# Second feed-forward layer from reduced-float32 parts to float16 parts, in a fused attention and rational feed-forward kernel

## The chip, the cores and the metric

The kernel runs on one core of one Trainium2 chip. The metric is the device time of one execution in microseconds (us); lower is better. The kernel before took 1280.21 us (median of three runs, 1277.5 to 1283.15).

## What is computed

The reference first computes an attention with a threshold over 8 batches x 8 heads x 576 tokens of 64 elements, then a feed-forward network whose activation is a ratio of two polynomials:

```python
scores = scale * np.matmul(q, k.transpose(0, 1, 3, 2))
thresh = np.max(scores, axis=-1, keepdims=True) - tau
scores = np.where(scores >= thresh, scores, -1000000000.0)
...
x = np.ascontiguousarray(attn_out.transpose(0, 2, 1, 3)).reshape(B * S, H * D)
...
h = x @ w_in
...
P = a[0] + a[1] * h + a[2] * h2 + a[3] * h3
Q = 1.0 + np.abs(b[0]) * np.abs(h) + np.abs(b[1]) * h2
g = P / (Q + 1e-06)
return (g @ w_out).astype(np.float32)
```

`x` has 4608 rows of 512, `w_in` is 512 x 2048, `w_out` 2048 x 512. Everything is float32 outside, so each float32 matrix product inside is either a whole float32 product or a sum of three cheaper products of high and low parts (high x high, low x high, high x low).

## The kernel before

**Attention.** Heads are taken in pairs; a *unit* is 128 query rows of a pair (or the last 64 rows, "short rows"). A unit multiplies queries with keys on TensorE (PE, L805 to L816), takes row maxima on VectorE (DVE, L822 or L824, one instruction a unit, 160 in all), applies threshold and exponential on ScalarE (ACT, L837 and L841), splits the probabilities into float16 high and low parts (`hi` on ACT or DVE through a helper, L326 or L328; `lo` on DVE, L863), transposes them by DMA and multiplies with V (L934). The result is `x`, again in high and low float16 parts (L944, L950). Units of batch 0 use plain float32 for this.

**Feed-forward.** Tokens are taken in chunks of 256 columns (two a batch, kind `m`; the 64 short rows of four batches together make a chunk of kind `r`): 18 chunks. A *step* takes one chunk and four blocks of 128 of the 2048 hidden units. Its first layer is 48 float16 products of 256 columns (`f_g1`, L1051). The activation works on tiles `t` of 128 x 1024: scaling out of PSUM (ACT, L1060), absolute value (L1065 or L1067), polynomials on DVE (L1071, L1074, L1084), logarithm (ACT, L1078) and exponential (ACT, L1081) for the reciprocal, a correction of the reciprocal on DVE (L1087, L1090) and the last product (L1093). The second layer (`f_g2`) adds into two PSUM banks of 128 x 512, one a half of the tokens: of four blocks, one is a whole float32 product a half (L1114) and three are products of three parts in the reduced float32 type `fp32r` (L1110). The parts of the activation are made block by block: a high part of 256 columns (`f_gh`, helper lines L318 on ACT, L320 on DVE) and a low part of 256 columns (`f_gl`, DVE, L1101), in tiles `g`. The program has 71 steps of four blocks and two of two blocks, 73 entries.

**Weights** come as 64-bit words and are decoded on the core during the first part of the program, in four groups of 512 hidden units. `w_in` is measured block by block (`junk`, L544 on ACT or L546 on DVE), a group's maximum goes through PE to all partitions (`scale_ops`, L422 to L440), and blocks are scaled and split into float16 halves (helpers L326 and L328, and L562). Of `w_out`, 4 of 16 blocks are decoded and kept; 12 are cast to `fp32r` (L318 or L320) and subtracted (L592).

**Order.** All operations are entered in a list with durations, due times and the buffers that they take; a planner (`Plan.order`) runs through them once at build time and writes each engine's instructions in the order in which they start in its plan. Where an operation may run on ACT or DVE (`FLEX`), the planner picks. Due times of steps come from `LEAD`, `SPACING` and their like; the list `LAST` names the chunks whose steps are due after all attention. Engines then run their own order and wait for one another by semaphores. Loads of q, k and v in later batches are issued from GpSimd's queue (POOL).

## Time and profile before

| what | value |
|---|---|
| median of the runs | 1280.21 us |
| the profiled execution itself | 1281.68 us |
| its span, first to last instruction | 1279.9 us |
| mean granted TensorE clock | 0.994 |
| time of the last max reduction's start (L822 or L824) | 1133 us |

The rows of the profile that the prediction rests on are shown there. A group's row gives line, engine, operation, tiles, shape and count, then its busy us and the mean ns of one, then the idle time before them and what ended it. Matmul records of whole float32 products come in twos. Rows of the table of stretches give a stretch, its length, and for each engine the busy us and the instructions in brackets, then the granted clock, the share of the DMA engines and GB/s.

### The profile page before, as it was taken

What the parts mean: (1) busy time and instruction counts of PE and PEld (TensorE: products, weight loads), DVE (VectorE), ACT (ScalarE), POOL (GpSimd) and SP (SyncE); (2) the same over time, 40 slices, a digit from 0 to 9 for tenths busy, and PEclk for the clock granted to TensorE, in tenths of its full rate; (3) what the DMA queues carried; (4) which work ended last, traced back from release to release, by engine and by line L of the source; (5) the groups of instructions that cost most, each with busy time, mean ns of one, the idle gap of its engine ahead of it and who ended that gap; (6) DMA issues with size and microseconds to landing.
All of it is one profiled execution on the core that took longest, in us unless ns stands there. A gap on an engine that the chain in (4) does not pass through costs nothing.

```text
span 1279.9 us, 25127 instructions
## 1 busy us (share of the span) xinstructions
PE 1246.4 (97%) x9252; PEld 889.8 (70%) x9252; DVE 1199.3 (94%) x1960; ACT 1074.5 (84%) x2180; POOL 231.3 (18%) x480
## 2 busy tenths in 40 slices
PE   8899999999999999999999999999999999999998
PEld 6576676676767667766667667677776667677775
DVE  5899999999999999999999899999999999997876
ACT  5999888989999888888897699999988998874454
POOL 2112000132132311332022140322121221100000
PEclk9999999999999999999999999999999999999999
DMA  7645246688667656776442765876566665530000
GB/s 216 174 143 163 78 105 112 134 144 154 105 133 132 146 107 119 142 137 126 91 105 56 131 141 111 142 135 136 104 120 125 130 123 112 111 71 17 18 17 17
DMA packets 338251, 146.64 MB, mean 115 GB/s; under 512 B 314416, under 2 KB 320720, under 8 KB 338128
## 3 DMA queue, kind: packets, MB, share of 16 engines
q1 hardware_dynamic: 316528, 87.67, 38.5%
q0 software_dynamic: 21280, 56.78, 16.4%
q8 instruction: 73, 1.20, 0.4%
q10 hardware_dynamic: 320, 0.59, 0.2%
q14 instruction: 50, 0.41, 0.1%
HBM read 60.30 MB, written 9.44 MB: 54 GB/s over the span
## 4 chain that ended last, share of the span: by engine, by line
PE 53%; DVE 27%; ACT 8%; issue 5%; DMA 3%; SPq 0%; DVEq 0%; ACTq 0%
PE banks L1051 16%; PE banks L1110 15%; PE banks L1114 6%; PE banks L934 6%; PE banks L816 5%; DVE e L863 4%; DVE st L822 3%; DMA pT<-e 2%; DVE t L1071 2%; DVE t L1087 2%; DVE t L1090 2%; PE banks L805 2%; DVE t L1084 2%; DVE t L1093 2%; DVE g L1101 2%
## 5 line engine op out<-in xcount | busy, mean ns | idle before, releaser
L1051 PEld LDWEIGHTS <-wi 128*128 128x128 f16 x3456 | 324.1, 98 | 144.1 <-issue 108.0
L1051 PE MATMUL banks<-x,wi 128*128 128x256 f16 x3072 | 374.7, 275 | 3.0 <-ACT t L1060 1.7
L1110 PE MATMUL banks<-wp,g 128*128 128x512 f32 x1296 | 355.2, 415 | 1.9 <-ACT g L318 1.2
L1110 PEld LDWEIGHTS banks<-wp,g 128*128 128x128 f32 x1296 | 234.0, 189 | 70.9 <-issue 15.5
L837 ACT ACTIVATE e<-banks,st 128x576 f32<-128x576 f32 x288 | 206.4, 735 | 18.5 <-DVE st L831 11.1
L841 ACT ACTIVATE e<-e,cf 128x576 f32<-128x576 f32 x288 | 221.0, 774 | 0.3
L863 DVE SCALAR_TENSOR_TENSOR e<-e,st,hi 128x576 f16<-128x576 f32 x252 | 203.5, 808 | 3.9 <-ACT hi L326 3.4
L822 DVE TENSOR_REDUCE st<-banks 128x2 f32<-128x1152 f32 x128 | 171.8, 1342 | 12.9 <-PE banks L816 10.8
L326 ACT ACTIVATE hi<-e,st 128x576 f16<-128x576 f32 x177 | 134.0, 769 | 51.9 <-DVE st L852 41.1
L816 PE MATMUL banks<-KK,QQ 64*128 64x512 f32 x512 | 144.5, 641 | 0.0
L1114 PE MATMUL banks<-wp,t 128*128 128x512 f32 x288 | 142.2, 608 | 1.7 <-DVE t L1093 1.6
L1060 ACT ACTIVATE t<-banks,hsc 128x512 f32<-128x512 f32 (+1 forms) x192 | 106.3, 575 | 25.9 <-PE banks L1051 24.7
L934 PEld LDWEIGHTS <-V 128*64 128x64 f16 x2520 | 104.1, 111 | 33.8 <-issue 32.6
L934 PE MATMUL banks<-pT,V 128*64 128x256 f16 (+1 forms) x2520 | 118.9, 249 | 3.0 <-DMA pT<-e 3.0
L1087 DVE SCALAR_TENSOR_TENSOR t<-t,co,t 128x1024 f32<-128x1024 f32 (+1 forms) x73 | 92.0, 1261 | 22.7 <-ACT t L1081 22.7
L1078 ACT ACTIVATE t<-t,co 128x1024 f32<-128x1024 f32 (+1 forms) x73 | 82.7, 1133 | 12.8 <-DVE t L1084 12.7
L1093 DVE SCALAR_TENSOR_TENSOR t<-t,co,t 128x1024 f32<-128x1024 f32 (+1 forms) x73 | 92.0, 1261 | 0.5
L1071 DVE SCALAR_TENSOR_TENSOR t<-t,co 128x1024 f32<-128x1024 f32 (+1 forms) x73 | 92.0, 1260 | 0.0
L1084 DVE SCALAR_TENSOR_TENSOR t<-t,co,t 128x1024 f32<-128x1024 f32 (+1 forms) x73 | 91.9, 1260 | 0.0
L1074 DVE SCALAR_TENSOR_TENSOR t<-t,co 128x1024 f32<-128x1024 f32 (+1 forms) x73 | 91.9, 1259 | 0.0
L1101 DVE TENSOR_TENSOR g<-t,g 128x256 fp32r<-128x256 f32 x216 | 86.6, 414 | 2.0 <-ACT g L318 1.6
L1090 DVE SCALAR_TENSOR_TENSOR t<-t,t 128x1024 f32<-128x1024 f32 (+1 forms) x73 | 87.7, 1201 | 0.4
(137 smaller groups left out, 1518.2 us busy)
## 6 DMA issues: line engine op xcount, KB each, us to landing
KK<-in_kT_dram POOLq DMA_DIRECT2D x84, 144.0 KB, 3.9
t<-in_w_in_dram POOLq DMA_DIRECT2D x16, 512.0 KB, 5.8
t<-in_w_out_dram POOLq DMA_DIRECT2D x16, 512.0 KB, 4.7
V<-in_v_dram POOLq DMA_DIRECT2D x24, 256.0 KB, 4.4
out_dram<-u POOLq DMA_DIRECT2D x24, 256.0 KB, 2.7
QQ<-in_qT_dram POOLq DMA_DIRECT2D x42, 144.0 KB, 3.1
QQ<-in_qT_dram POOLq DMA_DIRECT2D x42, 128.0 KB, 3.4
KK<-in_kT_dram SPq DMA_DIRECT2D x24, 144.0 KB, 3.5
```

Of the source, the lines that this page charges most:

```text
L326: nc.scalar.activation(dst, src, AF.Identity, scale=factor)
L816: nc.tensor.matmul(d, QQ[r, t * P:(t + 1) * P], KK[r, REM:S], **one)
L822: nc.vector.tensor_reduce(box["st"][:, 0:2], box["both"], AX.X, ALU.max, negate=True)
L837: nc.scalar.activation(ev(hh), box["s"][hh], AF.Prelu, scale=SCALE, bias=box["st"][:, 2 + hh:3 + hh], alpha=STEEP)
L841: nc.scalar.activation(e, e, AF.Exp, scale=passes, accum_out=box["st"][:, 4 + hh:5 + hh])
L863: nc.vector.scalar_tensor_tensor(box["lo"][:, c], ev(hh), box["st"][:, 6 + hh:7 + hh], box["hi"][:, c], ALU.mult, ALU.subtract)
L934: nc.tensor.matmul(dst, V[:, c * P + head * D:c * P + (head + 1) * D], rhs, start=c == 0 and n == 0, stop=c == NT and n == 2)
L1051: nc.tensor.matmul(d, wi_tile(c, f0 + j, hl), x[:, c, :], start=c == 0 and n == 0, stop=c == NC - 1 and n == 2)
L1071: nc.vector.scalar_tensor_tensor(box["r"], box["h"], a2, box["h"], ALU.add, ALU.mult)
L1087: nc.vector.scalar_tensor_tensor(box["q"], box["q"], qc, box["i"], ALU.add, ALU.mult)
L1110: nc.tensor.matmul(acc[tt], fr(g[:, x]), fr(wo[f][y]), start=begins and j == n == 0, stop=ends and j == nb - 1 and n == 2)
L1114: nc.tensor.matmul(acc[tt], box["r"][:, o:o + P], wo[f], start=begins and j == 0, stop=ends and j == nb - 1)
```

## The change

**Second layer.** `w_out` is now measured, scaled by group and split into float16 halves in the way of `w_in`; block 0 of each group is kept in scaled float32 as well (`wp`). In most steps block 0 stays a whole float32 product and the other three are three float16 products each; in the last 13 entries all four blocks are in float16 parts. The parts of the activation are made by one instruction for three blocks (768 columns) or for all four (1024).

**Scales.** For float16, the activation needs a scale that can't overflow. It is a bound: the greatest column norm of `w_in` (`f_columns`, four products of a row of ones with the squares, per group) times the scale of the chunk's rows goes through the polynomial's absolute coefficients (`f_bound` on POOL, `f_scales` on DVE), and its logarithm enters the exponential as a bias (`f_inv`). A run of steps of one kind and batch and group range has one such scale (12 runs). The correction (`f_n`) takes a tile's scalar where it had a constant, and the output's scale becomes `down`.

**Sizes.** Blocks of `w_in` and half of `w_out`'s groups are measured by a sum of squares on ACT, the rest by a maximum on DVE; V's batches 1 to 7 by squares on ACT.

**Order.** Only one chunk of the last batch is left in `LAST`, and short rows of batch 7 come with the first visit of its pairs. Eleven tiles `t` in place of eight; all times of the table and the planner's prices have other values.

```diff
+WHOLE, IN_PARTS = 1, 13
...
+STEPS = {'m': (4, 4, 4, 4), 'r': (4, 4, 4, 4), 'last': (4, 4, 4, 2, 2)}
+LAST = (1,)
+
+REST_FIRST = (7,)
...
-PARTS = 3
+SQUARES_W, SQUARES_V = (2, 3), (1, 2, 3, 4, 5, 6, 7)
...
-LEAD, SPACE0, SPACING = 4.776489494, 2.7365, 2.085146464
+LEAD, SPACE0, SPACING = 5.323779532, 2.637044739, 2.235134465
...
-    wo = [None] * NF
+    wo = wpool.tile([P, NW, NC, 2, WS], F16, name="wo")
+    wp = wpool.tile([P, NW, WHOLE, WS], F32, name="wp") if WHOLE else None
...
+            def size(n=n, box=box):
+                if plan.eng == "ACT":
+                    nc.scalar.activation(box["rw"][:, :, 0].bitcast(F32), box["w"], AF.Square, accum_out=wm[:, n:n + 1])
+                else:
+                    nc.vector.tensor_reduce(wm[:, n:n + 1], box["w"], AX.X, ALU.max, apply_absolute_value=True)
+            o7 = op({"ACT": 0.66} if squares else {"DVE": 0.62}, 0, key, size, [o6], (), [hold])
...
+        sd = scale_ops(key, lambda: wm[:, n:n + NC], 14 - o, inv, sc, [x[3] for x in pieces], AHEAD_RANK, squares, EVEN if o else MASK)
...
+            def f_columns():
+                for c, box, _, _ in pieces:
+                    nc.tensor.matmul(bank(hb), ones16, squared(box["rw"]), start=c == 0, stop=c == NC - 1)
...
+        for c, box, hold, _ in pieces:
+            def s1(c=c, box=box):
+                times(dst(c, 0), box["w"], sc)
+
+            def s2(c=c, box=box):
+                nc.vector.scalar_tensor_tensor(dst(c, 1), box["w"], sc, dst(c, 0), ALU.mult, ALU.subtract)
+            o1 = op(FLEX["s1"], 0, key, s1, [sd], (), [hold])
+            wd.append([op(FLEX["s2"], 0, key, s2, [o1], (), [hold])])
+            if o and c < WHOLE:
+                wd[-1].append(op(FLEX["s1"], 0, key, lambda c=c, box=box: times(wp[:, i, c], box["w"], sc), [sd], (), [hold]))
...
-        def f_wh(f=f, box=box):
-            copy(fr(wo[f][0]), box["w"])
-
-        def f_wl(f=f, box=box):
-            nc.vector.tensor_tensor(fr(wo[f][1]), box["w"], wo[f][0], ALU.subtract)
-        o = op(FLEX["wh"], 0, key, f_wh, [o], (), [hold])
-        wo_done.append(op("DVE", 0.66, key, f_wl, [o], (), [hold]))
...
+        if bb in REST_FIRST:
+            visits += [(v0 + i, half + rest) for i in range(NP - 1)] + [(v0 + NP - 1, half + rest + other)]
+            visits += [(v0 + i, other) for i in range(NP - 2, -1, -1)]
...
-        def f_inv():
-            nc.scalar.activation(box["i"], box["i"], AF.Exp, scale=-1.0)
+        def f_inv(x, j0, j1):
+            i = box["i"][:, j0 * CT:j1 * CT]
+            nc.scalar.activation(i, i, AF.Exp, scale=-1.0, bias=lnr(x))
...
-        def f_n():
-            nc.vector.scalar_tensor_tensor(box["q"], box["q"], -2.0, box["i"], ALU.add, ALU.mult)
+        def f_n(x, j0, j1):
+            q, i = (box[y][:, j0 * CT:j1 * CT] for y in "qi")
+            nc.vector.scalar_tensor_tensor(q, q, m2r(x), i, ALU.add, ALU.mult)
...
-        def f_gh(j):
-            box["g", j] = place(hg[j])
-            copy(fr(box["g", j][:, 0]), box["r"][:, j * CT:(j + 1) * CT])
-
-        def f_gl(j):
-            g = box["g", j]
-            nc.vector.tensor_tensor(fr(g[:, 1]), box["r"][:, j * CT:(j + 1) * CT], g[:, 0], ALU.subtract)
+        def f_gh(x, j0, j1):
+            box["g", x] = place(hg[x])
+            copy(box["g", x][:, 0, 0:(j1 - j0) * CT], box["r"][:, j0 * CT:j1 * CT])
+
+        def f_gl(x, j0, j1):
+            w = (j1 - j0) * CT
+            nc.vector.tensor_tensor(box["g", x][:, 1, 0:w], box["r"][:, j0 * CT:j1 * CT], box["g", x][:, 0, 0:w], ALU.subtract)
...
-            if in_parts(f):
-                g = box["g", j][:, :, tt * P:(tt + 1) * P]
-                for n, (x, y) in enumerate(((0, 0), (1, 0), (0, 1))):
-                    nc.tensor.matmul(acc[tt], fr(g[:, x]), fr(wo[f][y]), start=begins and j == n == 0,
-                                     stop=ends and j == nb - 1 and n == 2)
+            x = f // NC
+            if f % NC < whole:
+                o = j * CT + tt * P
+                nc.tensor.matmul(acc[tt], box["r"][:, o:o + P], wp[:, x, f % NC], start=begins and j == 0, stop=ends and j == nb - 1)
                 return
-            o = j * CT + tt * P
-            nc.tensor.matmul(acc[tt], box["r"][:, o:o + P], wo[f], start=begins and j == 0, stop=ends and j == nb - 1)
+            o = (f - max(x * NC, f0) - whole) * CT + tt * P
+            for n, (y, z) in enumerate(((0, 0), (1, 0), (0, 1))):
+                nc.tensor.matmul(acc[tt], box["g", x][:, y, o:o + P], wo[:, x, f % NC, z], start=begins and j == n == 0,
+                                 stop=ends and j == nb - 1 and n == 2)
...
+            def f_bound():
+                x = isx[:, b:b + 1] if kind == "m" else R
+                e = engines[plan.eng]
+                e.tensor_scalar(H, x, wmax, 1.0, ALU.mult, ALU.mult)
+                e.tensor_scalar(s, H, c2, H, ALU.add, ALU.mult)
+                e.tensor_scalar(s, s, c1, H, ALU.add, ALU.mult)
+                e.tensor_scalar(s, s, c0, ct, ALU.add, ALU.mult)
+
+            def f_scales():
+                nc.vector.scalar_tensor_tensor(s, H, c1s, s, ALU.add, ALU.min)
+                nc.vector.tensor_single_scalar(s.bitcast(I32), s.bitcast(I32), EVEN, ALU.bitwise_and)
+                nc.vector.tensor_scalar(s, s, SMALL, None, ALU.max)
+                nc.vector.tensor_scalar(R.bitcast(I32), s.bitcast(I32), -0.5, float(197 << 23), ALU.mult, ALU.add)
+                nc.vector.tensor_scalar(m2r, m2, R, None, ALU.mult)
+                nc.vector.tensor_scalar(down, s, dn, None, ALU.mult)
+
+            def f_ln_r():
+                nc.scalar.activation(lnr, m2r, AF.Ln, scale=-0.5)
...
+    order += [(x, 0, NF) for i, x in enumerate((("m", B - 1, 0), ("m", B - 1, 1), ("r", B // 4 - 1, 0))) if i not in LAST]
...
+    for i, (ck, f, nb, p, begins, ends, gs) in enumerate(todo):
+        moe_ops(ck, f, nb, p, begins, ends, i >= len(todo) - SOON, WHOLE if nb % NC == 0 and i < len(todo) - IN_PARTS else 0, gs)
```

How this moves instructions is seen at three places. First, ACT in the early part, while the weights of the second layer come in (`u`, `t`: decoding; `wp`, `wo`: weights; `e`, `pT`: attention). Before:

```order
L493 ACTIVATE u_78<-t_71 128x512
L499 ACTIVATE t_71<-t_71 128x512
L318 CAST wp_0_148<-t_73 128x512
L493 ACTIVATE u_76<-t_75 128x512
L318 CAST wp_0_150<-t_71 128x512
L499 ACTIVATE t_75<-t_75 128x512
```

The same stage of the changed kernel:

```order
L879 ACTIVATE e_73<-banks,st_81 128x576
L531 ACTIVATE u_70<-t_96 128x512
L339 ACTIVATE wo<-t_96,so 128x512
L331 COPY pT_76<-banks 128x4x128
L339 ACTIVATE wo<-t_99,so 128x512
L879 ACTIVATE e_73<-banks,st_81 128x576
L883 ACTIVATE e_73,st_81<-e_73,cf 128x576
```

A scaled half (`wo`), which waits for its group's scale (`so`), stands in the place of a cast, between the two exponential chains of a unit.

Second, DVE at the end of a group of the second layer's weights (`sc`: the group's maximum; `st`, `u<-ident`: attention). Before:

```order
L503 TENSOR_SCALAR u_76<-u_76 128x512
L333 ISA t_70<-t_70,u_78 128x512x2
L333 ISA t_74<-t_74,u_76 128x512x2
L320 CAST wp_0_155<-t_70 128x512
L427 TENSOR_SCALAR u_78<-ident,sc_95 128x128
L592 TENSOR_TENSOR wp_1_156<-t_70,wp_0_155 128x512
L592 TENSOR_TENSOR wp_1_158<-t_74,wp_0_157 128x512
```

In the changed kernel:

```order
L467 TENSOR_REDUCE sc_86<-banks 128x1
L469 TENSOR_SCALAR sc_86<-sc_86 128x1
L470 TENSOR_SCALAR sc_86<-sc_86 128x1
L474 TENSOR_SCALAR so<-sc_86 128x1
L476 RECIPROCAL so<-so 128x1
L1136 SCALAR_TENSOR_TENSOR t_94<-t_94,co 128x1024
L341 TENSOR_SCALAR wp<-t_96,so 128x512
L613 SCALAR_TENSOR_TENSOR wo<-t_96,so,wo 128x512
L613 SCALAR_TENSOR_TENSOR wo<-t_97,so,wo 128x512
L613 SCALAR_TENSOR_TENSOR wo<-t_99,so,wo 128x512
L613 SCALAR_TENSOR_TENSOR wo<-t_95,so,wo 128x512
```

The low parts of the four blocks now come together behind the chain that makes the group's scale.

Third, PE in the second layer of a step (`wp`, `wo`: weights; `g`: parts; `t`: whole activation). Before:

```order
L1110 MATMUL banks<-wp_0_145,g_97 128x512 x2
L1110 MATMUL banks<-wp_1_146,g_97 128x512
L1110 MATMUL banks<-wp_0_145,g_97 128x512 x2
L1110 MATMUL banks<-wp_1_146,g_97 128x512
L1114 MATMUL banks<-wp_147,t_74 128x512 x2
L812 MATMUL banks<-KK_115,QQ_113 128x2x64
```

In the changed kernel:

```order
L854 MATMUL banks<-KK_116,QQ_114 128x2x64
L858 MATMUL banks<-KK_116,QQ_114 128x512 x2
L1164 LDWEIGHTS g_89
L1164 MATMUL banks<-wo,g_89 128x512
L1164 LDWEIGHTS g_89
L1164 MATMUL banks<-wo,g_89 128x512
```

Each float16 product has a load of its own for its stationary part. Counted over the whole order, 1296 reduced-float32 products and 144 whole ones became 1368 float16 products and 120 whole ones. On DVE, 60 of the 73 entries begin ahead of the last max reduction before, and 61 in the changed kernel.

More of the change, by code (lines that the diff above doesn't have):

```diff
@@ L410, in masked_attention_rational_ffn, with bounds, scale_ops @@
     co = op("DVE", 2.1, 6.0, monic, [co])
-    def scale_ops(key, get, up, inv, s, after, ahead=0.0):
+    def bounds():
+        nc.vector.tensor_single_scalar(co_[:, 9:12].bitcast(I32), co_[:, 0:3].bitcast(I32), 0x7FFFFFFF, ALU.bitwise_and)
+        nc.vector.tensor_scalar(c1s, ct, 1.0, 0.25, ALU.add, ALU.mult)
+        nc.vector.scalar_tensor_tensor(c1s, c1s, c1, c2, ALU.mult, ALU.add)
+        nc.vector.scalar_tensor_tensor(c1s, c0, ct, c1s, ALU.mult, ALU.add)
+    co_b = op("DVE", 0.4, 6.0, bounds, [co])
+    def scale_ops(key, get, up, inv, s, after, ahead=0.0, squares=False, mask=MASK):
         box = {}
@@ L670, in is_plain @@
     def is_plain(bp, t):
-        return bp < NP and t in PLAIN
+        return t in PLAIN.get(bp, ())
     v_ops = {}
@@ L1028, in moe_ops, with can, slow, mid @@
         FW = nb * CT
+        parts = [(x, max(x * NC, f0) - f0, min(x * NC + NC, f0 + nb) - f0) for x in range(g, (f0 + nb - 1) // NC + 1)]
         box = {}
-        def can(kind):
-            return {e: size(e, d) for e, d in FLEX[kind].items() if e == "DVE" or not soon}
-        def size(e, d):
-            return d + (nb / 2 - 1) * (d - {"ACT": 0.18, "DVE": 0.08}[e])
-        def on(e, d, *rest):
-            return op(e, size(e, d), *rest)
+        def can(n, act, dve):
+            return {"DVE": dve(n)} if soon else {"ACT": act(n), "DVE": dve(n)}
+        def slow(n):
+            return 0.129 + n * 0.2667
+        def mid(n):
+            return 0.068 + n * 0.2667
+        def fast(n):
+            return 0.07 + n * 0.1333
+        def act(n):
+            return 0.098 + n * 0.2133
         bhs = [Hold("b", 1 if kind == "m" else 4, BH if p < end else BH + [(i,) for i in B3[0]]) for _ in range(nb // 2)]
@@ L1123, in f_o @@
                     o = o[:, tt * DM:(tt + 1) * DM]
-                nc.scalar.activation(o, acc[tt], AF.Identity, scale=osc)
+                nc.scalar.activation(o, acc[tt], AF.Identity, scale=down)
             obox[tt]["o"] = o
@@ new lines, in scale_of, with f_top @@
+    def scale_of(ck, gs):
+        kind, b, _ = ck
+        run = kind, b, gs
+        if run not in scales_of:
+            n = len(gs)
+            done, m2, wmax, dn = consts(gs)
+            tab = const.tile([P, 2 * n + 4], F32, name=f"gs_{kind}{b}_{gs[0]}_{n}")
+            m2r, lnr = tab[:, 0:n], tab[:, n:2 * n]
+            H, s, R, down = (tab[:, 2 * n + i:2 * n + i + 1] for i in range(4))
+            def f_top():
+                nc.vector.tensor_reduce(R, isx[:, 4 * b:4 * b + 4], AX.X, ALU.max)
+            def f_bound():
[14 more added lines that the diff above has]
+                nc.scalar.activation(lnr, m2r, AF.Ln, scale=-0.5)
+            bs = [b] if kind == "m" else range(4 * b, 4 * b + 4)
+            p = max(pos[(x * NP, 0)] for x in bs) + 1.5
+            rank, plan.rank = plan.rank, p
+            o = [done] + [isx_done[x] for x in bs]
+            if kind == "r":
+                o = [op("DVE", 0.08, p, f_top, o)]
+            o = op(BOUND, 0, p, f_bound, o)
+            o = op("DVE", 0.8, p, f_scales, [o])
+            o = op("ACT", 0.25, p, f_ln_r, [o])
+            plan.rank = rank
+            scales_of[run] = o, lnr, m2r, down
+        o, lnr, m2r, down = scales_of[run]
+        return o, lambda x: lnr[:, x - gs[0]:x - gs[0] + 1], lambda x: m2r[:, x - gs[0]:x - gs[0] + 1], down
```

318 lines of the change are left out of this document (178 added, 140 removed).

## The prediction

> **What bounds the kernel now.** I read the page first: the busy line, for which engines are near full.
>
> ```profile
> span 1279.9 us, 25127 instructions
> PE 1246.4 (97%) x9252; PEld 889.8 (70%) x9252; DVE 1199.3 (94%) x1960; ACT 1074.5 (84%) x2180; POOL 231.3 (18%) x480
> ```
>
> Two engines are nearly full and a third is not far off, so an average decides nothing. The second view is the table of stretches. I cut it where DVE starts its 8th, 16th, 24th and 32nd max reduction (62.6, 121.5, 184 and 241.2 us) and its last one, the 160th (1133 us), because the order of the changed kernel can be cut at the same places. Columns: length, then busy us (and instructions) of PE, weight loads, DVE, ACT, POOL.
>
> ```profile
> 0.00:62.60 62.60, 51.67 (x332) 38.57 (x334) 43.24 (x120) 47.47 (x105) 14.28 (x44) 0.97 0.69 198
> 62.60:121.50 58.90, 56.72 (x446) 41.46 (x443) 57.08 (x138) 57.81 (x125) 10.26 (x22) 1.00 0.48 142
> ...
> 241.20:1133.00 891.80, 880.74 (x6735) 620.32 (x6735) 865.15 (x1362) 789.76 (x1610) 201.24 (x403) 1.00 0.63 122
> 1133.00:1279.92 146.92, 140.86 (x898) 106.38 (x895) 117.11 (x146) 73.02 (x129) 0.00 (x0) 0.99 0.10 25
> ```
>
> Three stages with different limits. **Early**, with the weights decoded, ACT and DVE are both full (57.81 and 57.08 of 58.90). **Middle**: DVE 865.15 and PE 880.74 of 891.80; DVE has 26.7 us idle in all. **Tail** (the feed-forward steps left over when attention is done): PE has 6 us idle and DVE 29.8, so PE bounds it. The waits of DVE after 1133 us say the same: it stands waiting for the exponential, whose input comes from the product that PE has just made.
>
> ```profile
> DVE t L1087 <- ACT t L1081: 18.9, 10, 2.4
> ```
>
> Third, the chain that ended last gives the pace of each kind of product, where PE runs without a break (start, length, matmul records):
>
> ```profile
> 1132.92 9.17 PE banks L1051 x84
> 1142.09 1.72 PE banks L1114 x4
> 1145.12 2.80 PE banks L1110 x12
> ```
>
> First-layer float16 of 256 columns: 9.17/84 = 0.109 us. Whole float32: two records each, so 1.72/2 = 0.86 us a product. Reduced-float32 parts of 512 columns: 2.80/12 = 0.233 us.
>
> **The change, part by part.** Base: the profiled execution took 1281.7 us, span 1279.9; the median of the three runs is 1280.2, so I take 1.5 off at the end.
>
> *PE.* A full step (4 blocks, 2 token halves) costs 48 x 0.109 + 18 x 0.233 + 2 x 0.86 = 11.15 us now. No row has a float16 product of 512 columns. Its bounds: 0.109 (as for 256) and 0.233 (as the one it replaces); I take twice the 256-column row, 0.219, since both work row by row. Then a mixed step costs 5.23 + 18 x 0.219 + 1.72 = 10.9 (-0.25), and a step all in parts, which the last 13 entries are (12 full steps' worth), 5.23 + 24 x 0.219 = 10.5 (-0.65). The Trainium skill, "TensorE: Matmul & The Clock Gate", section "Back-to-back issue gap", gives 262 cycles for 256 columns and 518 for 512, about 216 ns, but also a sustained 131 ns for 512. Our row agrees with the first (0.109); by the second the step would cost 8.4 us.
>
> *Early: second-layer weights.* Counted in the order, over all weights: sizes of blocks on ACT 11 to 24, on DVE 5 to 8; scaled halves on ACT 6 to 22, on DVE 10 to 14; 16 new low halves on DVE for 12 subtractions; 12 casts (4 on ACT, 8 on DVE) go.
>
> ```profile
> L544 ACT ACTIVATE t<-t 128x512 f32<-128x512 f32 x11 | 7.6, 692 | 3.1 <-DVE t L333 3.1
> L544 ACT ACTIVATION_READ_ACCUMULATOR t<-t 128x1 f32 x11 | 2.3, 207 | 0.0
> L326 ACT ACTIVATE wi<-t,sw 128x512 f16<-128x512 f32 x6 | 4.6, 781 | 0.0
> L318 ACT CAST wp<-t 128x512 fp32r<-128x512 f32 x4 | 2.8, 688 | 0.3 <-DVE t L333 0.2
> L562 DVE SCALAR_TENSOR_TENSOR wi<-t,sw,wi 128x512 f16<-128x512 f32 x16 | 11.6, 745 | 0.0
> L592 DVE TENSOR_TENSOR wp<-t,wp 128x512 fp32r<-128x512 f32 x12 | 8.2, 683 | 0.1
> L320 DVE CAST wp<-t 128x512 fp32r<-128x512 f32 x8 | 3.5, 436 | 0.0
> L328 DVE TENSOR_SCALAR wi<-t,sw 128x512 f16<-128x512 f32 x10 | 4.5, 478 | 0.0
> L546 DVE TENSOR_REDUCE wm<-t 128x1 f32<-128x512 f32 x5 | 3.4, 680 | 0.0
> L427 DVE TENSOR_SCALAR u<-ident,sc 128x128 f32<-128x128 f32 x12 | 3.4, 281 | 0.0
> L437 DVE TENSOR_SCALAR sc<-sc 128x1 f32<-128x1 f32 x12 | 1.8, 153 | 0.4
> ```
>
> ACT: 13 x 0.90 + 16 x 0.78 - 2.8 = +21. DVE: 16 x 0.745 - 8.2 - 3.5 + 4 x 0.478 + 3 x 0.68 = +4.2; four more scale chains (two of 0.28 and five of 0.15 each), four column norms (0.68 and three of 0.15) and three tables of constants (seven of 0.15) are 5.3 + 4.6 + 3.2 = 13, in all +17. Together about +38, some 20 on each engine. Nothing hides it: both are full from 62.6 to 121.5. **+20 us**. Bounds: +10 if half of it finds the idle of the first 62.6 us (ACT 15, DVE 19), +40 if the two take turns. The added wait: no half of a group is written before all four blocks are sized and PE has broadcast their maximum; queued behind those halves on ACT are the exponentials of attention, and DVE waits for these. The bound of each run (four tiny operations on POOL) stands ahead of loads of q, k and v, in a queue that is 18% busy: nothing.
>
> *Middle, DVE.* How far instructions overlap is seen where three follow each other:
>
> ```profile
> 1184.70 1.28 DVE L1071 SCALAR_TENSOR_TENSOR t<-t,co 128x1024 f32<-128x1024 f32 x1
> ...
> 1185.90 1.28 DVE L1074 SCALAR_TENSOR_TENSOR t<-t,co 128x1024 f32<-128x1024 f32 x1
> ...
> 1187.09 1.28 DVE L1084 SCALAR_TENSOR_TENSOR t<-t,co,t 128x1024 f32<-128x1024 f32 x1
> ```
>
> They start 1.20 apart and last 1.28, so one costs its mean less 0.08. The rows touched:
>
> ```profile
> L1101 DVE TENSOR_TENSOR g<-t,g 128x256 fp32r<-128x256 f32 x216 | 86.6, 414 | 2.0 <-ACT g L318 1.6
> L320 DVE CAST g<-t 128x256 fp32r<-128x256 f32 x93 | 25.7, 285 | 2.2 <-PE banks L1110 1.5
> L318 ACT CAST g<-t 128x256 fp32r<-128x256 f32 x123 | 47.8, 401 | 41.9 <-PE banks L1110 35.7 <-DVE t L1093 5.3
> L1087 DVE SCALAR_TENSOR_TENSOR t<-t,co,t 128x1024 f32<-128x1024 f32 x71 | 90.5, 1276 | 22.7 <-ACT t L1081 22.7
> L1090 DVE SCALAR_TENSOR_TENSOR t<-t,t 128x1024 f32<-128x1024 f32 x71 | 86.3, 1215 | 0.4
> L328 DVE TENSOR_SCALAR hi<-e,st 128x576 f16<-128x576 f32 x75 | 38.0, 513 | 0.2
> L326 ACT ACTIVATE hi<-e,st 128x576 f16<-128x576 f32 x177 | 134.0, 769 | 51.9 <-DVE st L852 41.1
> ```
>
> Low parts: 216 of 256 columns become 60 of 768, 11 of 1024, 2 of 512. From 0.414 (256) and 0.683 (512, L592) the slope gives 0.95 and 1.22: 72.1 to 65.9, -6. High parts on DVE: 93 to 28 + 4 + 1, by 0.285 and 0.436, 19 to 17, -2 (ACT, by 0.401 and 0.688, -9). The step whose constant becomes a tile's scalar goes from L1090's price to L1087's: 73 x 0.06 = +4. High halves of attention, 18 fewer: -8 on DVE, +14 on ACT. Twelve runs' scales, six tiny operations each: +10. Copies and sizes of V that go to ACT: -3. Sum -5; the same addition over the order between max reductions 32 and 160 gives -13 for equal steps. I take -9. But one step more, 8.6 us (six at 1.2, low parts 0.87, part of the casts), stands ahead of the last max reduction (61 entries of 73, not 60): **0**.
>
> What PE's relief adds there is idle time that DVE loses: between 0 and 26.7. PE asks 52 x 0.25 = 13 less, and DVE waits where both queues interlock; I take **-10**.
>
> *Tail.* PE bounds it. 12 steps' worth stand behind the last max reduction now, 11 after: -11.15 - 11 x 0.65 = -18.3, and with PE's 6 idle kept, **-19**. DVE, 117.11 less a step, asks 108 and has some 20 left as cover. The new order of the last batch moves chunks, not work; that one step is all that it yields here, and the stores stay 30 on POOL's queue and 10 on SP's.
>
> Sum: 1281.7 + 20 + 0 - 10 - 19 = 1272.7, less 1.5: about **1272 us**.
>
> **The rivals.** *PE is the pace of the middle too, and the weights' work hides* (PE's 97% speaks for it, ACT's 57.81 of 58.90 against): all of PE's saving falls through, 1296 x 0.014 + (24 x 0.86 - 72 x 0.219) - 4 of added column sums = 19; 1261. *No gain in the middle*: DVE at 865 of 892 was the wall and keeps its idle: 1280.2 + 20 - 19 = 1281, no change. *Slower: the early stage takes turns.* Each group's maximum is one more round over DVE, PE and DVE, and while ACT scales halves, attention's exponentials stand still and DVE with them; the extra 40 us then add up in one line: 1280.2 + 40 - 19 - 10 = 1291, 1301 with no idle recovered. It decides from an early growth of 36 us (26 without recovery): the 32nd max reduction after 277 us instead of 241. *The product does not get cheaper*, 0.233 as before: the tail gives 15 instead of 19, 1276. *It gets far cheaper*, down to the 256-column row: the tail is left to DVE, 108 plus some 7 of waits in place of 127, 12 less: 1260. By the sustained 131 ns of the Trainium skill, "TensorE: Matmul & The Clock Gate", "Back-to-back issue gap", it would be near this one; no row here shows it.
>
> **How the numbers follow.** About 0.5%, 6.4 us, is what a measurement of this kernel can tell from no change: faster ends at 1273.8, slower begins at 1286.6. Forecast with its spread 1264 to 1277 (the idle recovered 5 to 18): 0.48, of which 0.34 lies below 1273.8. PE everywhere 0.14, far cheaper 0.03: faster 0.51. No gain in the middle, with the uncheaper product, 0.16, and 0.14 of the forecast's own: same 0.30. Taking turns 0.19. The range 1254 to 1290 leaves out most of the last and the lower edge of the second.
>
> **What would show it.** Right: the 32nd max reduction near 261 us; DVE's sum unchanged (1195 to 1210) with ACT 30 to 40 higher; float16 parts at 0.219; the last max reduction near 1143 and 127 us behind it. Wrong: an unchanged early stage (then 1261), over 277 us there (then 1291), or a middle that keeps its 27 us of DVE idle.

## The result, and the profile after

The changed kernel takes 1286.61 us (median of six runs, 1284.06 to 1290.67), the kernel before, run beside it on the same chip, 1279.51 us: ratio 1.0062, interval 1.0043 to 1.0081. It is slower by 0.6%; 1272 and faster were forecast.

The page of the changed kernel, for the busy line: against before PE has 12 us less, DVE 14 more, ACT 32 more.

```profile
span 1285.2 us, 25164 instructions
PE 1234.3 (96%) x9312; PEld 793.1 (62%) x9312; DVE 1212.9 (94%) x1878; ACT 1106.3 (86%) x2179; POOL 263.2 (20%) x532
```

The table of stretches, cut at the same max reductions as in the prediction (length, then busy us of PE, weight loads, DVE, ACT, POOL, the granted clock, DMA share and GB/s):

```profile
58.90:129.00 70.10, 63.95 (x500) 46.85 (x501) 67.33 (x181) 67.70 (x152) 11.63 (x23) 1.00 0.36 115
129.00:206.20 77.20, 70.83 (x512) 47.27 (x510) 72.47 (x170) 71.23 (x153) 10.94 (x28) 0.96 0.38 99
...
0.00:264.80 264.80, 239.92 (x1653) 161.60 (x1654) 236.82 (x531) 232.56 (x490) 36.63 (x98) 0.96 0.48 128
264.80:1161.70 896.90, 874.85 (x6848) 554.69 (x6846) 867.21 (x1243) 802.49 (x1583) 226.59 (x435) 0.99 0.63 122
1161.70:1285.24 123.54, 119.57 (x817) 76.86 (x814) 108.84 (x107) 71.22 (x107) 0.00 (x0) 1.00 0.12 28
```

Up to the 32nd max reduction 264.8 us instead of 241.2 (+23.6; forecast +20). The middle 896.9 instead of 891.8 (+5.1; forecast -10). The tail 123.5 instead of 146.9 (-23.4; forecast -19). The sum, +5.3, is the difference of the spans. The early and the tail term came out a little larger than forecast, in the direction forecast; the middle has the wrong sign. By the medians of all runs the kernel is 7.1 us longer; the profiled execution of the kernel before was 2 us above its median.

A note on the stretches: what is called the 8th, 16th, 24th and 32nd max reduction, here and ahead, is by the traces the one after it (the 9th, 17th, 25th and 33rd of 160), in all kernels alike, so the lengths compare as they stand.

The chain that ended last gives the prices in the tail (start, length, matmul records):

```profile
1162.17 0.86 PE banks L1160 x2
...
1214.88 10.48 PE banks L1099 x96
1225.36 5.18 PE banks L1164 x24
```

A float16 product of 512 columns paces at 5.18/24 = 0.216 us (0.219 was taken), one of 256 at 0.109, a whole one at 0.86. By the waits of DVE in the tail, what it stood waiting for there is mostly gone (18.9 us for the exponential before):

```profile
DVE t L1136 <- ACT t L1130: 3.8, 2, 2.5
```

### The profile page after: what moved, and what is told of

Its sections match the earlier page's. It is cut to its first block, busy times and chain, and to the rows that moved or that the text cites. A ratio compares the mean times of both kernels' runs of the same rounds, so it can differ in the third digit from the quotient of the medians.

```text
span 1285.2 us, 25164 instructions
## 1 busy us (share of the span) xinstructions
PE 1234.3 (96%) x9312; PEld 793.1 (62%) x9312; DVE 1212.9 (94%) x1878; ACT 1106.3 (86%) x2179; POOL 263.2 (20%) x532
## 5 line engine op out<-in xcount | busy, mean ns | idle before, releaser
L1099 PEld LDWEIGHTS <-wi 128*128 128x128 f16 x3456 | 334.0, 99 | 134.7 <-issue 85.0
L1099 PE MATMUL banks<-x,wi 128*128 128x256 f16 x3072 | 368.6, 275 | 16.0 <-ACT t L1108 12.7
L1164 PE MATMUL banks<-wo,g 128*128 128x512 f16 x1368 | 316.2, 380 | 3.4 <-DVE g L1151 3.4
L1164 PEld LDWEIGHTS <-g 128*128 128x128 f16 x1368 | 129.5, 98 | 179.1 <-issue 30.2
L864 DVE TENSOR_REDUCE st<-banks 128x2 f32<-128x1152 f32 x128 | 172.0, 1344 | 13.7 <-PE banks L858 12.5
L339 ACT ACTIVATE hi<-e,st 128x576 f16<-128x576 f32 x195 | 147.5, 768 | 42.1 <-DVE st L894 36.3
L858 PE MATMUL banks<-KK,QQ 64*128 64x512 f32 x512 | 147.9, 655 | 0.0
L1160 PE MATMUL banks<-wp,t 128*128 128x512 f32 x240 | 120.2, 611 | 1.6 <-ACT e L879 1.0
L687 POOL DMA_DIRECT2D QQ<-in_qT_dram x42 | 22.2, 527 | 336.8 <-PE banks L847 189.7
L1143 DVE SCALAR_TENSOR_TENSOR t<-t,co,t 128x1024 f32<-128x1024 f32 (+1 forms) x67 | 84.9, 1267 | 0.2
L1133 DVE SCALAR_TENSOR_TENSOR t<-t,co,t 128x1024 f32<-128x1024 f32 (+1 forms) x61 | 76.7, 1258 | 0.0
L1136 DVE SCALAR_TENSOR_TENSOR t<-t,co,t 128x1024 f32<-128x1024 f32 (+1 forms) x56 | 70.4, 1257 | 4.7 <-ACT t L1130 4.6
L1130 ACT ACTIVATE t<-t,gs_m 128x1024 f32<-128x1024 f32 (+1 forms) x65 | 73.3, 1128 | 0.5
```

What stands on the lines that cost most here:

```text
L339: nc.scalar.activation(dst, src, AF.Identity, scale=factor)
L858: nc.tensor.matmul(d, QQ[r, t * P:(t + 1) * P], KK[r, REM:S], **one)
L864: nc.vector.tensor_reduce(box["st"][:, 0:2], box["both"], AX.X, ALU.max, negate=True)
L1099: nc.tensor.matmul(d, wi_tile(c, f0 + j, hl), x[:, c, :], start=c == 0 and n == 0, stop=c == NC - 1 and n == 2)
L1160: nc.tensor.matmul(acc[tt], box["r"][:, o:o + P], wp[:, x, f % NC], start=begins and j == 0, stop=ends and j == nb - 1)
L1164: nc.tensor.matmul(acc[tt], box["g", x][:, y, o:o + P], wo[:, x, f % NC, z], start=begins and j == n == 0, stop=ends and j == nb - 1 and n ...
```

## The experiments

Eighteen kernels. Each keeps the order of the kernel that it starts from, unless "re-planned" is said: then the planner has written the order anew. Lines that only move the flag that ends a sum, or set a constant, are not shown in the code below. Lengths of the three stretches, in us, of each profiled execution; medians over runs, with the ratio to before in the same session (before's median was 1278.1 to 1280.5 in all):

| kernel | early | middle | tail | median | ratio to before |
|---|---|---|---|---|---|
| before | 241.2 | 891.8 | 146.9 | 1279.5 | |
| e1 less PE | 238.9 | 885.4 | 144.4 | 1269.7 | 0.9934 (0.9909 to 0.9959) |
| e2 less DVE | 236.0 | 890.7 | 145.9 | 1274.9 | 0.9969 (0.9952 to 0.9987) |
| e3 less ACT | 239.7 | 887.5 | 146.6 | 1278.2 | 1.0005 (0.9992 to 1.0017) |
| e5 less PE and DVE | 234.4 | 862.5 | 131.8 | 1229.1 | 0.9596 (0.9564 to 0.9627) |
| e13 PE -12 | 241.6 | 883.9 | 145.5 | 1273.2 | 0.9957 (0.9942 to 0.9972) |
| e14 DVE +17 | 241.2 | 906.5 | 150.5 | 1302.3 | 1.0186 (1.0164 to 1.0208) |
| e15 PE +12 | 242.0 | 897.1 | 149.4 | 1291.4 | 1.0107 (1.0087 to 1.0127) |
| e16 ACT more | 240.9 | 891.9 | 147.6 | 1282.2 | 1.0027 (1.0013 to 1.0041) |
| e8 more early work | 258.9 | 887.4 | 147.0 | 1295.3 | 1.0113 (1.0083 to 1.0142) |
| e9 new last order | 239.4 | 884.0 | 159.5 | 1284.6 | 1.0046 (1.0031 to 1.0061) |
| after | 264.8 | 896.9 | 123.5 | 1286.6 | 1.0062 (1.0043 to 1.0081) |
| e4 fewer weights | 262.4 | 896.4 | 123.6 | 1282.6 | 1.0036 (1.0024 to 1.0048) |
| e7 no split | 254.9 | 896.5 | 123.6 | 1276.5 | 0.9988 (0.9951 to 1.0025) |
| e6 less DVE | 263.9 | 893.3 | 123.7 | 1283.4 | 1.0026 (1.0008 to 1.0044) |
| e17 less ACT | 267.0 | 900.3 | 123.6 | 1287.5 | 1.0068 (1.0042 to 1.0095) |
| e18 PE -12 | 265.5 | 893.7 | 121.4 | 1282.0 | 1.0028 (1.0012 to 1.0043) |
| e10 old last order | 264.7 | 899.8 | 122.8 | 1289.4 | 1.0078 (1.0055 to 1.0101) |
| e11 no steps all in parts | 264.0 | 895.8 | 130.7 | 1292.1 | 1.0097 (1.0080 to 1.0115) |
| e12 halves on GpSimd | 280.8 | 896.2 | 123.5 | 1302.7 | 1.0181 (1.0161 to 1.0201) |

The middle was left as it is in e4, e7 and e12, and there it takes 896.2 to 896.5 us (896.9 in the changed kernel); e8, which leaves the middle of the kernel before as it is, has 887.4 (891.8). So one execution against one can differ by some 4 us, and smaller differences of a stretch decide little. The growth of the middle by the change (5.1 us) is not far above that, but it has the same sign, with 4 to 10 us, in every pair of these executions.

### What holds the middle of the kernel before (e1, e2, e3, e5)

Each takes work from one engine or two and leaves that part of the computation out: e1 the third product of each block in parts (PE), e2 the polynomial's last instruction (DVE), e3 the activation's second exponential (ACT), e5 both e1's and e2's.

```diff
-                for n, (x, y) in enumerate(((0, 0), (1, 0), (0, 1))):
+                for n, (x, y) in enumerate(((0, 0), (1, 0))):
```

```diff
 def f_r3():
-    nc.vector.scalar_tensor_tensor(box["r"], box["r"], a1, box["h"], ALU.add, ALU.mult)
+    pass
```

```diff
 def f_inv():
-    nc.scalar.activation(box["i"], box["i"], AF.Exp, scale=-1.0)
+    pass
```

> The kernel before with its order kept, but the third product of each reduced-float32 block (high activation x low weight) is left out: 432 products of 0.233 us, 100 us less on PE, nothing less on DVE and ACT. Theory W (the middle is walled by the work of DVE, with ACT close behind; relief of PE is worth nothing there): the stretch between max reductions 32 and 160 stays at 892 us within 10, DVE's idle time in it stays at 20 to 30, and only the tail gets shorter, by 12 steps x 6 x 0.233 = 17; in all 1258 to 1270. Theory P (DVE's idle time in the middle is caused by PE, as the prediction's -10 assumed): all 27 us of idle in the middle go, 865 to 875 there, in all 1238 to 1250. If PE sets the pace of the middle alone: 892 - 73 = 819 there, in all about 1190.

> The kernel before with its order kept, but one of the six polynomial instructions of a step on DVE (the third power's, L1084) is left out: 73 x 1.2 = 88 us less on DVE, 62 of them in the middle. Theory W: the middle gets shorter by 20 to 60 (until PE or ACT is next), the tail by 0 to 5 since PE bounds it; in all 1215 to 1260. If PE sets the pace of the middle alone: no change there, in all 1275 to 1281.

> The kernel before with its order kept, but the exponential that makes the reciprocal (ACT, L1081) is left out: 73 x 1.05 = 77 us less on ACT, 55 of them in the middle, nothing less on DVE and PE. Theory W with DVE alone as the wall: the middle stays at 892 within 10; the tail gets shorter by up to 10, since DVE waits 19 us for this instruction there. If ACT (790 of 892 busy) is a wall of its own or hands its lateness on to DVE: 20 to 40 shorter in the middle.

> The kernel before, with both removals together: the third product of each block in reduced-float32 parts on PE (432 fewer, some 100 us) and the polynomial's last instruction on DVE (73 fewer, some 88 us). Apart they gave -8.4 and -4 us. Twin walls (PE and DVE each hold the middle as soon as the other is relieved): together far more than the sum, the middle 40 to 60 us shorter than 891.8 and the whole 1215 to 1240 us. A third wall (waits, transposes by DMA, ACT): about the sum, the middle 880 or over and the whole 1260 to 1268.

The middle stretch in the table of stretches of e1, then of e2:

```profile
238.90:1124.30 885.40, 830.42 (x6419) 557.77 (x6416) 864.93 (x1363) 788.13 (x1610) 201.59 (x403) 1.00 0.66 123
```

```profile
236.00:1126.70 890.70, 879.82 (x6739) 620.79 (x6737) 813.60 (x1309) 790.68 (x1610) 201.07 (x403) 1.00 0.63 123
```

PE has 50 us less in e1 (880.7 to 830.4) and the stretch is 6.4 shorter; DVE has 52 less in e2 (865.2 to 813.6) and it is 1.1 shorter: within the scatter. The other engine stays where it was, at 865 and 880. In e5 both are down by 56 or 57:

```profile
234.40:1096.90 862.50, 823.73 (x6413) 556.40 (x6412) 809.45 (x1308) 784.27 (x1610) 201.19 (x403) 1.00 0.67 126
```

Now the stretch loses 29.3 us and the whole kernel 51.5, against 11.7 for the two apart. PE and DVE are two walls (engines that hold the time) of nearly one height. The middle did not fall by the 40 to 60 expected; that ACT (784) and the chains between engines come next is likely, but no run relieves all three. ACT alone (e3) gives 4.3 there, which is within the scatter, and nothing over the whole.

### What a change of the size at hand is worth there (e13, e14, e15, e16)

e13 leaves one product of 512 columns out of every step; e15 makes one twice (both change the sums of one block); e14 makes one low part of 256 columns twice on DVE, and e16 47 high parts twice on ACT.

```diff
                 for n, (x, y) in enumerate(((0, 0), (1, 0), (0, 1))):
+                    if tt == 0 and n == 2 and f % NC == 1:
+                        continue
```

```diff
-                for n, (x, y) in enumerate(((0, 0), (1, 0), (0, 1))):
+                parts = ((0, 0), (1, 0), (0, 1))
+                for n, (x, y) in enumerate(parts[:2] + parts[1:] if tt == 0 and f % NC == 1 else parts):
```

```diff
+            for _ in range(2 if (f0 + j) % NC == 1 else 1):
                 nc.vector.tensor_tensor(fr(g[:, 1]), box["r"][:, j * CT:(j + 1) * CT], g[:, 0], ALU.subtract)
```

```diff
+            for _ in range(2 if plan.eng == "ACT" and (f0 + j) % NC == 1 else 1):
                 copy(fr(box["g", j][:, 0]), box["r"][:, j * CT:(j + 1) * CT])
```

> The kernel before, same order, with one reduced-float32 product fewer in each step (72 fewer in all, 0.233 us each: 12 us of PE in the middle stretch, 3 in the tail), which is about the relief that the change gives PE in the middle. By the prediction's term such a relief is idle time that DVE loses: the middle 7 to 10 us under 891.8, the whole about 1267 to 1270. If PE and DVE are walls of equal height there: the middle 0 to 3 us shorter, the whole 0 to 4.

> The kernel before, same order, with one subtraction of 256 columns made twice in each step (0.335 us more of DVE a step: 17 us in the middle, 4 in the tail). If DVE's 26.7 us of idle in the middle can take it: 0 to 5 us longer in all. If the middle stands at equal walls, where added work counts nearly in full though removed work counts for nothing: the middle 12 to 17 us longer, the whole some 14 to 20.

> The kernel before, same order, with one reduced-float32 product more in each step (72 more, 12 us of PE in the middle, 3 in the tail). Equal walls: the middle 9 to 12 us longer, the whole 11 to 15. DVE the only wall of the middle: the middle at most 3 longer, the whole 3 to 6 by the tail.

> The kernel before, same order, with 47 of the high parts of 256 columns made twice on ACT (0.3 to 0.4 us each, some 14 to 19 us more of ACT in all, about as much as the change adds there in the middle). ACT has nearly 100 us idle in the middle stretch. If its added work hides: the middle within 2 us of 891.8, the whole within 3. If ACT is in the lockstep of PE and DVE: the middle 4 to 10 us longer, which would then explain the growth of the changed middle.

The middle stretch of e13, of e14 and of e16:

```profile
241.60:1125.50 883.90, 871.96 (x6680) 608.78 (x6677) 864.78 (x1362) 789.11 (x1610) 200.35 (x403) 1.00 0.64 123
```

```profile
241.20:1147.70 906.50, 889.88 (x6729) 616.59 (x6724) 886.94 (x1414) 790.94 (x1609) 200.43 (x403) 1.00 0.62 120
```

```profile
240.90:1132.80 891.90, 880.18 (x6734) 619.91 (x6734) 865.88 (x1362) 801.15 (x1642) 200.43 (x403) 1.00 0.62 122
```

PE 9 us less busy gives 7.9 in the middle. Over the whole it gives 5.6 by medians, between the two forecasts (8 to 11, and 0 to 4). So my own rival theory, nothing at equal walls, falls in the middle, and the prediction's way of turning PE's relief into DVE's idle holds roughly for the first few microseconds. Set beside e1, it also ends there: 50 us less gave 6.4 in the middle. The other direction has no such end: DVE 22 us more costs 14.7 in the middle and, with 28 more in all, 23.5 over the whole; PE some 10 more costs 5.3 there and, with 14 more in all, 12.6 over the whole. e15's 9 to 12 for the middle was missed, its 11 to 15 for the whole not. ACT's 11 us more cost nothing there; the whole of e16 is 3 us longer.

### Whether the early growth is the added work (e4, e7, e8)

e4 leaves out the measuring of the second-layer weights and their low halves (the products read the high halves twice); e7 leaves out their measuring, scaling and splitting, but for the float32 block of each group, and reads halves of the first layer's weights instead. Both keep the changed kernel's order. e8 adds work to the kernel before that no one waits for.

```diff
             def size(n=n, box=box):
+                if o:
+                    return
...
             def s2(c=c, box=box):
+                if o:
+                    return
```

```diff
             def s1(c=c, box=box):
+                if o:
+                    return
```

```diff
+            for _ in range(2):
+                nc.scalar.copy(box["rw"][:, :, 0].bitcast(F32), box["w"])
-            nc.vector.tensor_tensor(fr(wo[f][1]), box["w"], wo[f][0], ALU.subtract)
+            for _ in range(3):
+                nc.vector.tensor_tensor(fr(wo[f][1]), box["w"], wo[f][0], ALU.subtract)
```

(The first is e4, with the second e7, the third e8.)

> The changed kernel with its order kept, but the blocks of the second layer's weights are not measured (their sizes are a constant) and their low halves are not made (the products read the high halves twice): 8 sizes on ACT (7 us), 8 sizes and 16 low halves on DVE (17 us) less, all in the early part; PE does the same work, and the chains for the groups' scales stay. Theory W (the early part grew by the sum of the added work over two full engines): the 32nd max reduction comes 24/2 = 12 us sooner, about 253, and the whole is 10 to 14 shorter, 1273 to 1277. Rival T (it grew because each group's scale is waited for, a round over DVE, PE and DVE, with ACT and DVE taking turns): the chains are still there, so under 5 us are won. Rival N (what is won early is lost to a later wait): the 32nd max reduction sooner, the whole the same.

> The changed kernel without all of the second-layer weights' new early work: its blocks are neither measured nor scaled into halves (only block 0 of each group still is, in float32), and the products read halves of the first layer's weights instead. Some 17 us of ACT and 20 of DVE go early, more than the change had added on DVE. If the early growth is this work on two full engines: the 32nd max reduction 15 to 20 us earlier than 264.8 and the whole as much shorter, about 1268. If the growth lies in the order and the chains of waits, which this kernel keeps: at most 5 us.

> The kernel before with early work added that no one waits for: for each of the 12 blocks of the second layer in parts two more copies of the block on ACT and two more subtractions on DVE, some 16 us on each engine, in the same order. If both engines are full and work there counts in full: the 32nd max reduction 14 to 18 us later than 241.2 and the whole 12 to 18 longer, about 1294. If holes of the early stage take it: under 5 us.

The early stretch of e8, then of e7:

```profile
0.00:258.90 258.90, 229.65 (x1623) 164.45 (x1623) 233.32 (x480) 226.10 (x467) 29.45 (x77) 0.97 0.50 131
```

```profile
0.00:254.90 254.90, 234.02 (x1653) 158.92 (x1654) 221.81 (x506) 219.06 (x461) 35.28 (x98) 0.99 0.50 133
```

e8: DVE +16.3 and ACT +14.4 on 217.0 and 211.7 make the stretch 17.7 longer: early, work on both engines counts in full. e7: DVE 15.0 and ACT 13.5 less than in the changed kernel give 9.9 back, and 10 over the whole. e4: DVE 13.7 less, ACT only 5.1 less, gives 2.4, where 12 were expected. That looks like one of two walls lowered, here with ACT as the other. Expected were 15 to 20 of e7, so not all of the growth falls with that work. What is left of it stands beside what e7 keeps: 4.8 us of added work on DVE and 7.4 on ACT, the new order, and the chains of waits. These were not told apart.

### Whether the tail is the parts or the new last order (e9, e10, e11)

e9 is the kernel before with the changed order of the last batch; e10 the changed kernel with the old one; e11 the changed kernel with a mixed step everywhere. All three are re-planned.

```diff
-LAST = (0, 1, 2)
+LAST = (1,)
+REST_FIRST = (7,)
```

```diff
-LAST = (1,)
+LAST = (0, 1, 2)
-REST_FIRST = (7,)
+REST_FIRST = ()
```

```diff
-WHOLE, IN_PARTS = 1, 13
+WHOLE, IN_PARTS = 1, 0
```

> The kernel before with the changed order of the last batch alone (one chunk in the list LAST instead of three, short rows of batch 7 with the first visit of its pairs), its tables otherwise as they were; 59 entries instead of 60 begin ahead of the last max reduction. If the shorter tail of the change (-23.4 us) came from this order: the tail 15 us or more under 146.9. If it came from the step fewer behind the last max reduction and the cheaper parts, as the prediction has it: the tail 8 to 14 us longer than 146.9 (one entry more) and the whole within 6 us of before.

> The changed kernel with the old order of the last batch (three chunks in LAST, short rows of batch 7 with the second visit), its tables otherwise as they are, and so re-planned. If the new order of the last batch moves chunks and not work, as the prediction has it: the stretch up to the 32nd max reduction as in the changed kernel (265), the whole within 8 us of 1286.6. If that order carries the tail's gain: 10 to 20 us longer.

> The changed kernel with a whole float32 product for block 0 in all full steps, the last 13 entries too, and so re-planned. By the prediction a step all in parts is 0.40 us cheaper on PE than a mixed one (10.5 against 10.9): some 11 steps behind the last max reduction make the tail 4 to 5 us longer, about 128, and the whole 1291. If DVE bounds the tail by now, whose parts get shorter here (768 columns instead of 1024): no change, within 2 us.

The order alone lengthens the tail by 12.6 (one entry more stands in it) and the kernel by 6; without it the changed kernel keeps its tail (122.8 against 123.5) and is 2.8 longer. The steps all in parts are worth 7.2 in the tail and 5.5 in all, more than the 4 to 5 of the count: PE has 5.0 less (124.56 in e11), the rest is idle time. So the tail's gain is the step fewer and the cheaper parts, as the prediction had it. Where the step fewer comes from it had wrong: it said that "the new order of the last batch" yields it, but that order alone puts one entry more behind the last max reduction, and e10, without it, has a tail of the same length.

### What the changed middle waits for (e6, e17, e18), and an attempt at a better kernel (e12)

e6, e17 and e18 are the twins of e2, e3 and e13 in the changed kernel, with the same lines left out.

> The changed kernel without the polynomial's last instruction on DVE (some 88 us fewer, 62 of them in the middle). If the change has made DVE the only wall of the middle, since PE asks less there: 20 to 60 us off the middle's 896.9. If PE is still the equal of DVE, as before the change, where the same removal took 1 us off the middle and 4 off the whole: 2 to 6 us off the whole.

> The changed kernel without the second exponential of the activation on ACT (some 77 us fewer). The same removal left the kernel before as it was (middle -4.3, whole -2). If ACT, with 802 us in the middle after the change, holds the middle: 8 us or more off the middle's 896.9. If it does not: 2 to 5.

> The changed kernel with one float16 product fewer in each step (72 fewer, 0.22 us each: 12 us of PE in the middle). In the kernel before the same relief gave 7.9 us in the middle and 5.6 in all. If PE is still as much a wall there after the change: 5 to 9 us off the middle. If the change has already used up what relief of PE is worth: 0 to 3.

DVE's 56 us less take 3.6 off the middle and 3.2 off the whole; PE's 8 less take 3.2 and 4.6; ACT's 50 less take nothing off (the profiled execution of e17 was the longest of its four). None of the three, relieved alone, gives back more than 5 us. ACT's 13 us more are not what made the middle longer: taking 50 off gives nothing here, and adding 11 cost nothing in e16.

e12 keeps all of the computation and makes the halves of 12 second-layer blocks on GpSimd.

```diff
             def s1(c=c, box=box):
+                if o and c >= WHOLE:
+                    nc.gpsimd.tensor_scalar(dst(c, 0), box["w"], sc, 1.0, ALU.mult, ALU.mult)
+                    nc.gpsimd.tensor_scalar(box["w"], box["w"], sc, 1.0, ALU.mult, ALU.mult)
+                    nc.gpsimd.tensor_tensor(dst(c, 1), box["w"], dst(c, 0), ALU.subtract)
+                    return
```

> The changed kernel with the float16 halves of 12 of the 16 second-layer blocks made on GpSimd (three instructions a block) instead of ACT and DVE: some 13 us off DVE and 5 off ACT in the early stage, and all of the computation is kept. If these engines are the early walls and GpSimd's queue has room: the 32nd max reduction 5 to 8 us earlier than 264.8 and the whole about 1280, the equal of before. If GpSimd's instructions are long, or hold up the loads behind them in its queue: no earlier, or later by up to 20 us.

It is 16 us later at the 32nd max reduction. GpSimd's group of instructions by line in the early stage, then DVE's:

```profile
L613 POOL TENSOR_TENSOR wo<-t,wo 128x512 f16<-128x512 f32 x12 | 15.8, 1316 | 1.0
L611 POOL TENSOR_SCALAR wo<-t,so 128x512 f16<-128x512 f32 x12 | 12.2, 1018 | 22.6 <-DVE so L476 11.2 <-issue 7.8 <-ACT e L886 3.5
```

```profile
L620 DVE SCALAR_TENSOR_TENSOR wo<-t,so,wo 128x512 f16<-128x512 f32 x4 | 4.9, 1220 | 0.0
L341 DVE TENSOR_SCALAR wp<-t,so 128x512 f32<-128x512 f32 x4 | 3.8, 946 | 0.0
```

GpSimd waits 11.2 us for DVE's scales with the loads of the next weights behind it, and DVE's own halves take 1220 and 946 ns where they took 744 and 480 in the changed kernel. What each has of the 16 us was not told apart. None of the kernels that keep the whole computation beats the kernel before.

## Why the prediction was wrong

**Early, right.** +23.6 against +20; ACT +20.9 (21 counted), DVE +19.8 (17 counted). Where some of the rest comes from is seen at one place. ACT, then PE, in the time line of the changed kernel at the end of a group's scale (start, length, [idle time before and its releaser]):

```profile
130.92 2.69 ACT L339 ACTIVATE wo<-t,so 128x512 f16<-128x512 f32 x4
133.52 0.56 ACT L331 COPY pT<-banks 128x512 f32<-128x512 f32 x1
```

```profile
134.14 1.16 PE L928 MATMUL banks<-u,e 128*128 128x128 f32 x8 [1.51 <-ACT pT L331]
136.13 0.69 PE L933 MATMUL banks<-u,e 128*64 128x128 f32 x4 [0.83 <-ACT pT L331]
```

Four scaled halves run on ACT ahead of the copy that PE waits for, and the granted clock then is 0.50 from 136 to 142 us: four matmul records of a whole product (L1160) take 3.78 us there. In e7, without these halves, the clock is 1.00 over the same stretch, and the same four records take 1.98; in e4, which keeps the halves, it falls too (0.50 in 134 to 140 us). The kernel before has a fall of its own near there, but a shorter one (0.66 in 140 to 145 us). It is the rival of the early stage that takes turns, but at one place, not in the sum: its condition, the 32nd max reduction after 277 us, was not met.

**Tail, right.** -23.4 against -19. PE has 21.3 us less (140.86 to 119.57; 18.3 counted) and 4.0 idle instead of 6.1. The price of the parts and PE as the wall of the tail were right; the origin of the step fewer was not (see e9 and e10).

**Middle, wrong.** DVE's busy time came near its term (+2.0 against 0). The step that failed is "What PE's relief adds there is idle time that DVE loses ... PE asks 52 x 0.25 = 13 less ... I take -10": DVE's idle went from 26.7 to 29.7, where 16.7 was forecast. Seen from PE, the middle is 5.9 us less of work and 11.0 more of idle time (11.1 to 22.1). Two things stand in the place of that step.

First, the relief was not there. The term for DVE counted the one step more ahead of the last max reduction (8.6 us), the term for PE did not. With it PE asks 53 x 10.9 - 52 x 11.15 = 2 less, not 13; its busy time fell by 5.9. The trace has both sides: the second layer's products there cost some 19 us less at the measured paces (970 parts at 0.233 and 106 whole at 0.86 before, 954 at 0.216 and 107 whole after), but the first layer has 110 products more (2494 weight loads before, 2604 after), 12 us at 0.109. e9, where one entry fewer lies ahead of the last max reduction, prices such a step in the middle at 7.8 us. e13 shows what a relief of PE is worth when it is there (7.9 us for 9), so the conversion was about right and its input wrong. By that conversion 5.9 us would still have been worth some 5; DVE's idle grew by 3.0 instead.

Second, the prediction put the bound of each run at "nothing", since it "stands ahead of loads ... in a queue that is 18% busy". By the waits of PE in the middle, the changed kernel has holes that the kernel before has not. Each row gives who waited for whom, then us in total, times, and the longest; first the kernel before, waiting for ACT's reading of the first layer's banks, then the changed kernel:

```profile
PE banks L1051 <- ACT t L1060: 1.7, 2, 1.4
```

```profile
PE banks L1099 <- ACT t L1108: 11.3, 3, 5.6
...
PE banks L1164 <- DVE g L1151: 3.4, 2, 2.9
```

The largest, in the time lines of ACT (the second output `u` is made), POOL, ACT and PE:

```profile
894.30 0.67 ACT L1175 ACTIVATE u<-banks,gs_m 128x512 f32<-128x512 f32 x1
```

```profile
895.66 1.05 POOL L1305 TENSOR_SCALAR gs_m<-isx,gc 128x1 f32<-128x1 f32 x1
...
899.44 0.91 POOL L1308 TENSOR_SCALAR gs_m<-gs_m,co 128x1 f32<-128x1 f32 x1
900.29 1.15 POOL L1184 DMA_DIRECT2D out_dram<-u  x2
```

```profile
903.98 1.55 ACT L339 ACTIVATE u<-V,sx 128x640 f16<-128x640 f32 x2 [4.08 <-DMA out_dram<-u]
...
908.00 0.67 ACT L1108 ACTIVATE t<-banks,hsc 128x512 f32<-128x512 f32 x1
```

```profile
908.71 4.00 PE L1099 MATMUL banks<-x,wi 128*128 128x256 f16 x18 [5.61 <-ACT t L1108]
```

The bound's four tiny operations take 4.7 us on POOL (895.66 to 900.35); behind them in its queue stands the store of the outputs `u`, the second of which was finished at 894.97; ACT needs that buffer for the next V and stands 4.08 us; behind it stands the reading of the banks for which PE waits 5.61. My estimate: without the bound ahead of it the store would start 4.6 us earlier, and ACT's wait would be gone. A second hole is at 471 us (4.45): there the bound of the short rows' run stands behind three loads of V, and DVE waits for POOL, then ACT for DVE's chain of scales:

```profile
468.54 0.22 DVE L1311 SCALAR_TENSOR_TENSOR gs_r<-gs_r,co 128x1 f32<-128x1 f32 x1 [1.35 <-POOL gs_r L1308]
```

A third, of 2.94, is at 1051.8 us, behind the same chain. The three are 13.0 us of PE's time, and the granted clock falls behind the first two, as the table of stretches has it (it stands third from the end of a row):

```profile
470.00:475.00 5.00, 3.92 (x13) 1.86 (x13) 4.23 (x6) 5.00 (x10) 0.00 (x0) 0.51 0.49 93
475.00:480.00 5.00, 5.00 (x38) 4.08 (x38) 5.00 (x7) 3.53 (x6) 3.65 (x7) 0.80 0.45 125
...
905.00:910.00 5.00, 1.29 (x7) 0.89 (x7) 3.56 (x6) 5.00 (x10) 0.00 (x0) 0.70 0.20 41
910.00:915.00 5.00, 5.00 (x24) 3.07 (x23) 2.83 (x5) 3.67 (x8) 0.11 (x1) 0.61 0.55 82
```

In e17 and e18 the first two stand at the same places (4.41 and 5.63 in e17). That the holes are there and what released each is shown by the trace; that they are what made the middle longer is argued from it, since no kernel with the bound moved to another queue was run. Taken unit by unit, at every fourth max reduction, the changed kernel's lag behind the kernel before grows by some 5.4 us across each of the three places (449 to 485, 886 to 925 and 1031 to 1065 us); but it grows by 5.0 at one other place and falls by up to 9.6, since the two orders differ, so this supports the reading and doesn't settle it. They may also be why PE's relief gave 3.2 us in e18 and 7.9 in e13, though that difference is hardly above the scatter.

**The rivals.** "No gain in the middle" (1281) came nearest in its outcome for that stage; its ground, DVE as the wall, did not hold (52 us less of DVE took 1.1 off in e2), and it lacked the new holes. "PE is the pace of the middle too" fell with e1 (50 us less of PE took 6.4 off), and the weights' work did not hide. "The early stage takes turns" (1291) is as near in time as "no gain", but not by its mechanism: the early stage grew by 23.6 where it needed 36. One slip changes little: the prediction's terms add up to 1271.2, given as 1272. The cheaper product came out as taken (0.216 against 0.219), so both rivals on its price fell; the sustained 131 ns of the Trainium skill ("TensorE: Matmul & The Clock Gate", "Back-to-back issue gap") is not reached here, its 216 ns is.

## What to carry to other kernels

Where two engines are near full, the price of an edit has two sides: most of the added work counts on either one (23.5 us for 28 of DVE in e14, 12.6 for 14 of PE in e15), removed work only until the other engine holds (in the middle 9 us less of PE: 8 back; 50 less: 6 back), and large gains need both lowered together (e5: 51 where the two apart gave 12). When a step moves from one stage to another, move it in the account of every engine. And a tiny operation can cost what stands behind it in its queue: follow the store or the load behind it to the buffer that it frees, and to who waits for that.
